# Windowed attention feeding a SwiGLU block: two groups moved one unit, one output from the PE to the crossbar, and a copy ahead of a load

## The chip, the cores and the metric

The kernel runs on one core of a Trainium2 chip. The metric is the device time of one execution in microseconds (us). The kernel before was run 8 times: median 239.15 us, from 238.8 to 240.25. One execution more was profiled.

The engines are named as in the profile: PE is TensorE (PEld its weight loads), DVE is VectorE, ACT is ScalarE, POOL is GpSimd, SP is SyncE, which here only issues DMAs.

## The reference

Attention over a sink of 4 keys and a causal window of 128 keys, for 4 batches, 8 heads, 768 tokens and a head size of 64; then a SwiGLU block over all 3072 tokens, with 512 model columns and 1536 inner columns. Inputs and output are float32.

```python
def _attn_ref(q, k, v, n_sink, window):
    scores = scale * np.matmul(q, k.transpose(0, 1, 3, 2))
    keep = is_sink | in_window          # key < 4, or 0 <= query - key < 128
    scores = np.where(keep, scores, -1000000000.0)
    a = np.exp(scores - np.max(scores, axis=-1, keepdims=True))
    a = a / (np.sum(a, axis=-1, keepdims=True) + 1e-09)
    return np.matmul(a, v)

x = attn_out.transpose(0, 2, 1, 3).reshape(B * S, H * D)
g = x @ w_gate
out = (g / (1 + np.exp(-g)) * (x @ w_val)) @ w_out
```

## The kernel before

**Two tilings.** Attention works on 12 *groups* of 256 tokens, three to a batch (`g`, with `b, c = divmod(g, 3)`; `c == 0` is the start of a batch, which has no sink step and no keys before it). The SwiGLU block works on 8 *blocks* of tokens (`tb`) of the sizes 256, 256, 256, 512, 512, 512, 512, 256 (L42). Their first tokens (`OFF`) are 0, 256, 512, 768, 1280, 1792, 2304 and 2816. So block 3 holds groups 3 and 4, block 4 groups 5 and 6, block 5 groups 7 and 8, block 6 groups 9 and 10.

**Steps of attention for a group.** Four loads bring k and q of both 128-token halves as bfloat16 into the tile `nat` (L111, POOL), two bring v into `va` (L122, POOL); the two together are `NV(g)`. From group 4 on `nat` has one buffer (`natp`, L62), so the loads of a group wait until the transposes of the group before have read it. `xbar(g)` (L253) transposes the four pieces by DMA on SP into `kT` and `qT` (L259). For groups 2 and 3 `step_TN` does this on the PE. `step_S` (L277, twice for each group, four heads each) makes 8 to 12 score matmuls (L292) into four PSUM banks, and four exponentials on ACT (L299); its mask multiply on DVE (L304) is put off in the list `later`. `step_K` (L308) makes scores and the exponential against the sink keys. `step_PV` (L338, four for each group: 2 halves of the tokens by 2 halves of the heads) multiplies with v (L355) and puts off a reciprocal (L363) and a multiply (L369) on DVE, which write `xn`. `step_X` (L377, two for each group) transposes `xn` into the block's input `xT`: on the PE with a copy by DVE or ACT for the groups in `PEX` (L45; L396, L403, L399), by a DMA on SP for the others (L391). `flush` (L210) emits what stands in `later`.

**Units of the SwiGLU block.** A `gate` unit (L448) makes the gate matmuls `pg` (L417), the tanh on ACT (L432), then the attention steps woven into it, then the value matmuls `pv` (L417) and two DVE operations, `u` (L438) and `ht` (L444), and flushes. A `down` unit (L462) makes 12 matmuls (L475) for 128 tokens, with the attention steps spread between them and a flush after each, then a copy by ACT (L480) and the output's DMA on SP (L483).

**What sets the order.** Every engine works in program order, and the program order is written out by hand: `weave` (L513) walks over a list of units and hands to unit *i* the steps that `slots` has for it, in the order in which they are listed. SP and POOL issue their DMAs in this order too, and wait at each one until what it needs is there. PSUM has 8 banks in one pool (`psum`, L74), each new tile taking the bank that has been free longest.

The units that the change touches:

- first weave (L654): units 0 to 11 are gates of blocks 0 and 1, 12 to 17 the six gates of block 2, 18 and 19 the downs of block 0, 20 and 21 of block 1, 22 and 23 of block 2. Into units 14 to 22 groups 3 and 4 are woven
- second weave (L677), block 3: units 0 to 11 are its gates, 12 to 15 its downs. Groups 5 and 6 are woven in by `pair(5, 6)` (L669), which places the steps of two groups by unit, all shifted by `sh` where that is given
- the weaves after that (L681, L684) use `pair(7, 8)` and `pair(9, 10)` without a shift

Of the kernel before, what the change touches and what calls it, by code (L numbers as in the profile page):

```python
# [14 lines left out]
def kernel(  # L15
# [12 lines left out]
    nc = tc.nc  # L28
# [13 lines left out]
    SIZES = [256, 256, 256, 512, 512, 512, 512, 256]  # L42
    assert sum(SIZES) == NTOK and NG == 12
    OFF = [sum(SIZES[:i]) for i in range(len(SIZES))]
    PEX = (0, 1, 2, 4)  # L45

    VS = 72
    FCH = [2] * 6
# [108 lines left out]
    warmed = const.tile([P, 1], FP32)  # L157
# [49 lines left out]
    kTs, qTs, es_t, e_t, xns, xTs = {}, {}, {}, {}, {}, {}  # L207
# [171 lines left out]
    def step_X(g, j, evict="v"):  # L379
# [6 lines left out]
        elif tb > 1 and off == 0:  # L386
            xTs[tb] = dense(xtp.tile([P, DMC * 512], BF16, tag="xT", name="xT"),
                            DMC, SIZES[tb])
        if g not in PEX:
            def sp():  # L390
                nc.sync.dma_start_transpose(xTs[tb][:, :, off:off + P], xns[g, j])  # L391
# [97 lines left out]
    def gates(tb):  # L489
        return [(gate, tb, f) for f in range(0, DFC, 512 // SIZES[tb])]  # L490

    def downs(tb):
        return [(down, tb, t) for t in range(SIZES[tb] // P)]

    def A(fn, *a):
        return lambda: fn(*a)

    def TN(g, evict="av"):
        return [A(step_TN, g, i, j, evict) for j in range(2) for i in range(2)]

    def Ss(g):
        return [A(step_S, g, p2) for p2 in range(2)]

    def PVs(g):
        return [A(step_PV, g, j, hh) for hh in range(2) for j in range(2)]

    def Xs(g):
        return [A(step_X, g, j) for j in range(2)]

    def K(g):  # L510
        return A(step_K, g)

    def weave(us, slots):  # L513
        assert all(i < len(us) for i in slots)
        for i, (fn, tb, x) in enumerate(us):
            fn(tb, x, slots.get(i, []))
# [7 lines left out]
    def slots(*pairs):  # L524
        sl = {}
        for at, steps in pairs:
            for i, step in zip(at if isinstance(at, tuple) else (at,) * len(steps),
                               steps):
                sl.setdefault(i, []).append(step)
        return sl  # L530
# [114 lines left out]
    def L(*fs):  # L645
        def f():
            for x in fs:
                x()
        return f

    def NV(g):
        return L(A(load_nat, g), A(load_v, g))

    weave(us, slots(  # L654
        (0, [K(1)]), (1, [A(step_PV, 1, 0, 0), A(step_PV, 1, 0, 1, "a"), A(step_PV, 1, 1, 0),
                              A(step_PV, 1, 1, 1, "a"), flush]),
        (2, [A(step_X, 1, 0, "a"), A(step_X, 1, 1, "now")]),
        ((4, 4, 5, 5), TN(2)), ((6, 7), Ss(2)), (6, [K(2)]),
        ((8, 8), PVs(2)[:2]), (9, [A(step_PV, 2, 0, 1, "a"), A(step_PV, 2, 1, 1, "a")]),
        ((10, 11), [A(step_X, 2, 0, "a"), A(step_X, 2, 1, "a")]),  # L660
        (11, [NV(4), lambda: nc.gpsimd.tensor_copy(out=vcl[64:128], in_=vcl[0:64])]), ((14, 14, 15, 15), TN(3, "aa")),
        (15, [A(xbar, 4)]), (15, [NV(5)]), (19, [A(xbar, 5)]), (19, [NV(6)]),
        (23, [A(xbar, 6)]), (23, [NV(7)]),
        ((17, 18), Ss(3)), (18, [A(step_ks, 1)]), (18, [A(step_vsb, 1)]),
        ((19, 19, 19, 20), PVs(3)), (20, Xs(3)),
        ((19, 20), Ss(4)), (19, [K(4)]),
        ((21, 21, 22, 22), PVs(4)), (22, Xs(4))))

    def pair(ga, gb, sh=0):  # L669
        s = sh  # L670
        return [((s, s + 2), Ss(ga)), (s, [K(ga)]),
                ((s + 4, s + 5, s + 6, s + 7), PVs(ga)),
                ((s + 6, s + 8), Ss(gb)), ((s + 8, s + 9), Xs(ga)), (s + 6, [K(gb)]),
                ((12, 12, 13, 13) if s else (10, 10, 11, 12), PVs(gb)),
                ((14, 14) if s else (12, 13), Xs(gb))]

    weave(gates(3) + downs(3), slots(  # L677
        (2, [A(xbar, 7)]), (2, [NV(8)]),
        (15, [A(step_ks, 2), A(step_vsb, 2)]), *pair(5, 6),
        (15, [A(xbar, 8)]), (15, [NV(9)])))  # L680
    weave(gates(4) + downs(4), slots(  # L681
        *pair(7, 8), (3, [A(xbar, 9)]), (15, [A(step_ks, 3), A(step_vsb, 3)]),
        (3, [NV(10)]), (15, [A(xbar, 10)]), (15, [NV(11)])))
    weave(gates(5) + downs(5), slots(*pair(9, 10), (6, [A(xbar, 11)])))  # L684
    us = gates(6) + gates(7) + downs(6) + downs(7)
    us[-1] = (lambda tb, t, a: down(tb, t, a, True), *us[-1][1:])
# [37 lines left out]
```

## Time and profile before

| | us |
|---|---|
| median of 8 runs | 239.15 |
| the profiled execution | 238.8 |
| its span, first to last instruction | 236.9 |
| PE busy | 229.1 |
| DVE busy | 158.6 |
| ACT busy | 114.6 |
| POOL busy | 74.5 |

The profiled execution lies at the low end of the 8 runs; its span is 1.9 us shorter than its time. The table of windows gives the engines by stage. Each row has the stretch in us from the span's start, its length, the busy time and number of instructions of each engine, the granted clock of the PE, the busy share of DMA (not used here), and the GB/s moved.

```profile
43.25:55.16 11.91, 11.91 (x120) 10.46 (x120) 8.41 (x14) 6.13 (x12) 4.73 (x6) 1.00 2.10 152
55.16:75.37 20.21, 19.80 (x179) 10.10 (x181) 11.85 (x33) 9.63 (x21) 8.05 (x10) 1.00 1.18 123
75.37:101.53 26.16, 25.85 (x198) 12.48 (x201) 22.03 (x44) 14.72 (x30) 9.46 (x12) 1.00 1.45 143
101.53:111.27 9.74, 9.69 (x53) 4.55 (x53) 3.12 (x10) 1.79 (x3) 3.50 (x5) 1.00 1.85 187
```

The five busy columns are PE, PEld, DVE, ACT and POOL. The first row is units 12 to 17 of the first weave, the second its downs, the third the gates of block 3, the fourth its downs. The PE is busy in all of them, at the full clock. DVE is busiest in the gates, 22.03 of 26.16 us.

### The profile page before, as it was taken

To read this page: it belongs to the slowest core of one execution; us is meant where nothing else is said; L and a number is where in the kernel's file an instruction comes from. 1 tells how busy PE (TensorE), PEld (TensorE's weight loads), DVE (VectorE), ACT (ScalarE), POOL (GpSimd) and SP (SyncE) were. 2 spreads that over 40 slices of the span, in tenths; PEclk is the share of its full clock that TensorE was granted. 3 is DMA by queue.
4 is the path that set the end of the run, shared out by engine and by line. 5 is a ranking of instruction groups with operands and counts; after the bars stand their busy time and mean duration, and the time that the engine had idled before them with its cause. 6 is when DMAs were issued, how large, how long until landed. Compare 5 with 4: busy or idle time off the path is not lost.

```text
span 236.9 us, 4886 instructions
## 1 busy us (share of the span) xinstructions
PE 229.1 (97%) x1874; PEld 127.3 (54%) x1901; DVE 158.6 (67%) x335; ACT 114.6 (48%) x237; POOL 74.5 (31%) x98
## 2 busy tenths in 40 slices
PE   8899999999999999999999999999999999999994
PEld 5567845795554444544445454444554445488443
DVE  5998788768652888960898980698970598877000
ACT  5796485467452836412846522655622663333221
POOL 8995875720807126170260800080000000000000
DMA  8999999993999989999499994599214100200132
GB/s 140 155 179 178 180 200 206 158 149 73 134 136 201 174 114 117 150 117 220 112 113 130 104 80 153 135 90 140 43 21 142 59 3 0 44 3 1 52 127 89
DMA packets 107655, 27.36 MB, mean 115 GB/s; under 512 B 94704, under 2 KB 104688, under 8 KB 107632
## 3 DMA queue, kind: packets, MB, share of 16 engines
q0 software_dynamic: 76640, 13.90, 77.1%
q1 hardware_dynamic: 30448, 12.89, 26.7%
q8 instruction: 15, 0.25, 0.4%
q10 hardware_dynamic: 544, 0.26, 0.4%
q14 instruction: 8, 0.07, 0.1%
HBM read 28.34 MB, written 6.29 MB: 146 GB/s over the span
## 4 chain that ended last, share of the span: by engine, by line
PE 88%; ACT 4%; DVE 2%; DMA 2%; issue 2%; POOL 0%; DVEq 0%; ACTq 0%; POOLq 0%
PE pd L475 26%; PE pv L417 26%; PE pg L417 25%; PE o L355 4%; PE s L292 4%; DMA x<-in_q_dram 2%; ACT e L299 2%; PE pn L245 1%; ACT xn L366 1%; ACT e L572 1%; PE o L335 1%; PE pk L320 1%; ACT th L432 1%; DVE u L438 1%; PE px L396 0%
## 5 line engine op out<-in xcount | busy, mean ns | idle before, releaser
L438 DVE SCALAR_TENSOR_TENSOR u<-th,pg 128x512 bf16<-128x512 f32 x72 | 49.1, 682 | 38.7 <-ACT th L432 38.7
L417 PE MATMUL pg<-xT,wg 128*128 128x512 bf16 (+1 forms) x351 | 73.1, 335 | 0.7
L417 PE MATMUL pv<-xT,wv 128*128 128x512 bf16 (+1 forms) x351 | 73.0, 336 | 0.7 <-ACT e L299 0.2
L432 ACT ACTIVATE th<-pg 128x512 f32<-128x512 f32 x72 | 43.5, 603 | 62.3 <-PE pg L417 58.5
L475 PE MATMUL pd<-wo,ht 128*128 128x512 bf16 (+2 forms) x291 | 64.8, 370 | 0.4
L444 DVE TENSOR_TENSOR ht<-u,pv 128x512 bf16<-128x512 bf16 x66 | 45.4, 687 | 10.4 <-PE pv L417 3.5
L417 PEld LDWEIGHTS <-wg 128*128 128x128 bf16 x360 | 35.0, 98 | 28.1 <-issue 0.7
L299 ACT ACTIVATE e<-s 128x512 bf16<-128x512 f32 (+1 forms) x88 | 42.7, 581 | 3.5 <-PE s L292 3.5
L475 PEld LDWEIGHTS <-ht 128*128 128x128 bf16 x300 | 27.9, 98 | 30.0 <-issue 0.5
L417 PEld LDWEIGHTS <-wv 128*128 128x128 bf16 x360 | 32.0, 98 | 20.9 <-issue 1.7
L111 POOL DMA_DIRECT2D nat<-in_k_dram x20 | 17.6, 888 | 75.2 <-DMA qT<-nat 72.9
L480 ACT ACTIVATE ot<-pd 128x512 f32<-128x512 f32 (+1 forms) x24 | 14.3, 596 | 47.4 <-PE pd L475 43.4
L304 DVE TENSOR_TENSOR e<-e,mask 128x1024 bf16<-128x1024 bf16 (+1 forms) x44 | 27.4, 657 | 3.9 <-ACT e L299 3.9
L122 POOL DMA_DIRECT2D va<-in_v_dram x24 | 21.5, 914 | 5.4 <-DMA wo<-in_moe_w_out_dram 2.5
L369 DVE TENSOR_TENSOR xn<-o,rcp 128x256 bf16<-128x256 f32 x44 | 18.7, 424 | 1.5
L355 PEld LDWEIGHTS <-e 128*128 128x128 bf16 x352 | 15.0, 98 | 8.0 <-DVE lt L603 0.4
L111 POOL DMA_DIRECT2D nat<-in_q_dram x20 | 17.7, 899 | 1.0 <-DMA wv<-in_moe_w_val_dram 0.4
L355 PE MATMUL o<-va,e 128*128 128x65 bf16 x352 | 17.0, 193 | 0.4 <-DVE lt L603 0.3
L292 PE MATMUL s<-qT,kT 64*128 64x128 bf16 (+1 forms) x240 | 12.9, 237 | 0.0
L292 PEld LDWEIGHTS <-kT 64*128 64x128 bf16 x240 | 7.7, 94 | 7.6 <-issue 6.6
L482 DVE TENSOR_SCALAR ot<-pd 128x128 f32<-128x128 f32 x1 | 0.3, 291 | 14.3 <-PE pd L475 14.3
L363 DVE RECIPROCAL rcp<-o 128x4 f32<-128x4 f32 x48 | 8.1, 174 | 1.4 <-PE o L355 1.3
(73 smaller groups left out, 91.9 us busy)
## 6 DMA issues: line engine op xcount, KB each, us to landing
out_dram<-ot SPq DMA_DIRECT2D x23, 256.0 KB
va<-in_v_dram POOLq DMA_DIRECT2D x24, 128.0 KB, 6.4
nat<-in_k_dram POOLq DMA_DIRECT2D x20, 128.0 KB, 5.1
nat<-in_q_dram POOLq DMA_DIRECT2D x20, 128.0 KB, 5.7
wg<-in_moe_w_gate_dram POOLq DMA_DIRECT2D x6, 256.0 KB, 7.8
wv<-in_moe_w_val_dram POOLq DMA_DIRECT2D x6, 256.0 KB, 8.6
wo<-in_moe_w_out_dram POOLq DMA_DIRECT2D x4, 384.0 KB, 11.1
st<-in_q_dram ACTq DMA_DIRECT2D x2, 128.0 KB
```

Of the source, the lines that this page charges most:

```text
L111: nc.gpsimd.dma_start(x[:, i, j].rearrange("p (h d) -> p h d", d=D), src[b, :, t0:t0 + P].rearrange("h p d -> p h d"))
L122: nc.gpsimd.dma_start(va[:, j, :, 0:D], v[b, :, t0:t0 + P].rearrange("h p d -> p h d"))
L292: nc.tensor.matmul(pss[2 * pp + h][:, col:col + n], kTs[b][r, p, kk:kk + P], qTs[b][r, p, qq:qq + n], start=True, stop=True)
L299: nc.scalar.activation(e_t[g][:, h0 + h, lo:512], pss[2 * pp + h][:, lo:512], AF.Exp, scale=scale)
L304: nc.vector.tensor_tensor(e, e, m[:, :, lo:512].broadcast_to([P, 2, 512 - lo]), op=ALU.mult)
L355: nc.tensor.matmul(o, l, r, start=(c == 0 and i == 0), stop=(i == len(mms) - 1), skip_group_check=True)
L369: nc.vector.tensor_tensor(xn, po[:, :, 0:D], rcp.broadcast_to([P, 4, D]), op=ALU.mult)
L417: nc.tensor.matmul(ps[:, i * n:(i + 1) * n], ws[fi][:, c, fo * P:(fo + 1) * P], xTs[tb][:, c], start=(c == 0), stop=(c == DMC - 1))
L432: nc.scalar.activation(th, pg, AF.Tanh, scale=0.5)
L438: nc.vector.scalar_tensor_tensor(u, th, 1.0, pg, op0=ALU.add, op1=ALU.mult)
L444: nc.vector.tensor_tensor(hts[tb][:, f:f + 512 // SIZES[tb]].rearrange("p a n -> p (a n)"), u, pv, op=ALU.mult)
L475: nc.tensor.matmul(po, hts[tb][:, f, ts * P:(ts + 1) * P], wos[f // n][:, f % n, lo:hi], start=(f == 0), stop=(f == DFC - 1))
```

## The change

It has four parts.

1. `PEX` loses group 4: its output goes to `xT` by two DMA transposes on SP instead of eight PE transposes and two DVE copies.
2. In the first weave the scores, PVs and outputs of groups 3 and 4 stand one unit sooner (scores at units 16 and 17, then 18 and 19). K(4) now stands behind group 4's second scores. `xbar(5)` and `NV(6)` move from unit 19 to unit 22.
3. `xbar(6)` and `NV(7)` move from unit 23 of the first weave to unit 1 of the second, `xbar(7)` from unit 2 to unit 8 of the second, `NV(8)` from unit 2 to unit 13. Groups 5 and 6 are woven in with a shift of one unit, where `pair` now gives other places for the second group's PVs (10, 11, 11, 12) and outputs (12, 13).
4. Ahead of `NV(8)` stand a flush and `behind(3)`: POOL copies one element of `xTs[3]`, in its last column, to the scratch tile `warmed`.

```diff
--- before.py
+++ after.py
@@ -42,7 +42,7 @@
     SIZES = [256, 256, 256, 512, 512, 512, 512, 256]
     assert sum(SIZES) == NTOK and NG == 12
     OFF = [sum(SIZES[:i]) for i in range(len(SIZES))]
-    PEX = (0, 1, 2, 4)
+    PEX = (0, 1, 2)
 
     VS = 72
     FCH = [2] * 6
@@ -506,6 +506,10 @@
 
     def Xs(g):
         return [A(step_X, g, j) for j in range(2)]
+
+    def behind(tb):
+
+        nc.gpsimd.tensor_copy(out=warmed[0:1], in_=xTs[tb][0:1, 0, 511:512])
 
     def K(g):
         return A(step_K, g)
@@ -659,25 +663,24 @@
         ((8, 8), PVs(2)[:2]), (9, [A(step_PV, 2, 0, 1, "a"), A(step_PV, 2, 1, 1, "a")]),
         ((10, 11), [A(step_X, 2, 0, "a"), A(step_X, 2, 1, "a")]),
         (11, [NV(4), lambda: nc.gpsimd.tensor_copy(out=vcl[64:128], in_=vcl[0:64])]), ((14, 14, 15, 15), TN(3, "aa")),
-        (15, [A(xbar, 4)]), (15, [NV(5)]), (19, [A(xbar, 5)]), (19, [NV(6)]),
-        (23, [A(xbar, 6)]), (23, [NV(7)]),
-        ((17, 18), Ss(3)), (18, [A(step_ks, 1)]), (18, [A(step_vsb, 1)]),
-        ((19, 19, 19, 20), PVs(3)), (20, Xs(3)),
-        ((19, 20), Ss(4)), (19, [K(4)]),
-        ((21, 21, 22, 22), PVs(4)), (22, Xs(4))))
+        (15, [A(xbar, 4), NV(5)]),
+        ((16, 17), Ss(3)), (18, [A(step_ks, 1), A(step_vsb, 1)]),
+        ((18, 18, 18, 19), PVs(3)), (19, Xs(3)),
+        ((18, 19), Ss(4)), (19, [K(4)]),
+        ((20, 20, 21, 21), PVs(4)), (21, Xs(4)), (22, [A(xbar, 5), NV(6)])))
 
     def pair(ga, gb, sh=0):
         s = sh
         return [((s, s + 2), Ss(ga)), (s, [K(ga)]),
                 ((s + 4, s + 5, s + 6, s + 7), PVs(ga)),
                 ((s + 6, s + 8), Ss(gb)), ((s + 8, s + 9), Xs(ga)), (s + 6, [K(gb)]),
-                ((12, 12, 13, 13) if s else (10, 10, 11, 12), PVs(gb)),
-                ((14, 14) if s else (12, 13), Xs(gb))]
+                ((10, 11, 11, 12) if s else (10, 10, 11, 12), PVs(gb)),
+                ((12, 13), Xs(gb))]
 
     weave(gates(3) + downs(3), slots(
-        (2, [A(xbar, 7)]), (2, [NV(8)]),
-        (15, [A(step_ks, 2), A(step_vsb, 2)]), *pair(5, 6),
-        (15, [A(xbar, 8)]), (15, [NV(9)])))
+        (1, [A(xbar, 6), NV(7)]), (8, [A(xbar, 7)]), *pair(5, 6, 1),
+        (13, [flush, A(behind, 3), NV(8)]),
+        (15, [A(step_ks, 2), A(step_vsb, 2), A(xbar, 8), NV(9)])))
     weave(gates(4) + downs(4), slots(
         *pair(7, 8), (3, [A(xbar, 9)]), (15, [A(step_ks, 3), A(step_vsb, 3)]),
         (3, [NV(10)]), (15, [A(xbar, 10)]), (15, [NV(11)])))
```

## The prediction

> **What bounds the kernel now.** I read the page first (busy shares, chain of waits), then TensorE's order of time around the change, then the orders of time of SyncE and GpSimd, last the completion marks of the transfers (16 for each transfer in the trace).
>
> ```profile
> span 236.9 us, 4886 instructions
> PE 229.1 (97%) x1874; PEld 127.3 (54%) x1901; DVE 158.6 (67%) x335; ACT 114.6 (48%) x237; POOL 74.5 (31%) x98
> PE 88%; ACT 4%; DVE 2%; DMA 2%; issue 2%; POOL 0%; DVEq 0%; ACTq 0%; POOLq 0%
> ```
>
> TensorE is the chain, and "busy" alone doesn't prove it full, so I looked at starts. From 43 us on a 128x512 matmul follows the last one every 0.216 us; the steps of attention between them cost what they cost. I found two real stalls: 0.17 us after group 6's scores at 89.28 us and 0.24 us at 126.26 us. So what a reordering can still win is TensorE work taken out, plus at most 0.4 us.
>
> ```profile
> 71.25 0.39 PE L396 MATMUL px<-ident,xn 128*128 128x128 bf16 x4
> 71.47 0.59 PE L475 MATMUL pd<-wo,ht 128*128 128x512 bf16 x2
> 71.91 0.39 PE L396 MATMUL px<-ident,xn 128*128 128x128 bf16 x4
> 72.13 3.40 PE L475 MATMUL pd<-wo,ht 128*128 128x512 bf16 x14
> 75.37 1.03 PE L417 MATMUL pg<-xT,wg 128*128 128x512 bf16 x4
> 89.28 0.50 PE L292 MATMUL s<-qT,kT 64*128 64x256 bf16 x8
> 111.27 1.03 PE L417 MATMUL pg<-xT,wg 128*128 128x512 bf16 x4
> ```
>
> Group 4's two PE transposes hold TensorE from 71.25 to 71.47 and from 71.91 to 72.13: 0.22 us each. 75.37 is unit 0 of the weave of block 3, 111.27 that of block 4.
>
> ```profile
> 62.97 1.21 SPq L259 DMA_TRANSPOSE kT<-nat  x1
> 64.84 1.27 SPq L259 DMA_TRANSPOSE qT<-nat  x1
> ...
> 69.45 3.49 SPq L391 DMA_TRANSPOSE xT<-xn  x2
> ...
> 105.16 1.25 SPq L391 DMA_TRANSPOSE xT<-xn  x1
> ```
>
> SyncE issues in order, about 1.3 us for each transpose. Group 3's output waits behind group 5's four input transposes, which wait for loads.
>
> ```profile
> 59.10 1.75 POOL L111 DMA_DIRECT2D nat<-in_k_dram  x2 [9.61 <-DMA qT<-nat]
> 72.57 1.75 POOL L111 DMA_DIRECT2D nat<-in_k_dram  x2 [8.21 <-DMA qT<-nat]
> 87.62 1.76 POOL L111 DMA_DIRECT2D nat<-in_k_dram  x2 [9.81 <-DMA qT<-nat]
> 99.78 1.75 POOL L111 DMA_DIRECT2D nat<-in_k_dram  x2 [6.89 <-DMA qT<-nat]
> ```
>
> There is one `nat` buffer. A group's loads start when the last transpose of the group before has landed; these four lines are one chain, 13.5, 15.1 and 12.2 us a step. By the marks group 4's transposes land at 58.55, group 5's at 72.01, group 6's at 87.07, group 7's at 98.94, about 0.55 us ahead of each line.
>
> **What the Trainium skill says.** "DMA: Bandwidth & Descriptors", section "Issuing engines are not separate DMA queues": transfers of all queues share the same 16 DMA engines. The trace agrees: with nothing beside it a 128x512 transpose lands 2.4 us after its issue (140.13 to 142.53); group 6's second output transpose, issued at 105.16 with group 8's six loads ahead, takes 6.0 and lands at 111.15, 0.12 us before TensorE wants it. "TensorE: Matmul & The Clock Gate", "Part 4: PE-mode transpose", gives about 275 ns for one in a kernel; here the records last 219 ns but follow each other every 56, and 56 is what is saved. "Perfetto Trace Analysis", "DMA Instruction — SWDGE (GPSIMD)": a GpSimd DMA's record ends with its descriptors, not the data; so I use marks for landings (3.4 to 7.5 us after issue for loads here), not the 0.9 us records.
>
> **The change, part by part.**
>
> *Group 4's output by the crossbar.* Eight PE transposes go: 8 x 0.055 = -0.44 us on the path. Two vector copies of 0.42 us go too, beside TensorE, worth nothing. Two SyncE transposes come: 1.2 us each to issue, 2.4 to land.
>
> *Groups 3 and 4 a unit sooner.* TensorE's work stays. Units 16 and 17 each take one score step of group 3 (0.53 us), so unit 18 starts at 55.16 + 0.53 = 55.69 us. Its six steps put group 4's first scores at matmul 10: 55.69 + 10 x 0.216 + 0.12 + 0.25 + 0.12 (PVs) + gaps of 0.1 = 58.45, against 60.82 before. They need group 4's last transpose, landed at 58.55: 0.1 us of stall. ScalarE then has 4 exps (2.06 us), the output copy (0.6), 4 exps, and only then the exp of K(4), which now stands after the second scores: 59.05 + 2.06 + 0.5 + 2.4 + 0.17 = about 64.2, while TensorE reaches the sink matmuls of PV(4) at about 64.07: another 0.2 with the handover. Masks (0.55 and 0.69 us) and PSUM banks free up ahead of need.
>
> Group 4's last xn is ready near 68.9, its transposes issue at 68.3 and 69.6 and land by 72; unit 0 of block 3 comes at 75.37 - 0.44 + 0.3 = about 75.1. Three us spare: hidden.
>
> *Group 5's crossbar from unit 19 to 22.* On SyncE it now follows unit 21's output (ScalarE copy at about 70.5, issue to 71.4). Its `nat` is there long before, so four issues 1.31 apart, 71.45 to 75.4, plus 2.45 in a quiet stretch: landed at 77.85. Group 5's scores are moved a unit too, to unit 1: 75.1 + 1.73 + 0.96 = 77.8 (0.96 from 75.37 to 76.33). Level: 0 to 0.5, I take 0.15. Behind the waiting scores stand unit 1's other matmuls, then ScalarE and VectorE.
>
> *Loads and crossbar of groups 6 and 7.* GpSimd starts group 6's loads at 77.85 + 0.55 = 78.4, 5.8 us later than before. A quiet chain step from start of loads to the last landing is 11.3 us (87.62 to 98.94), the others 12.9 and 14.5. With 12.1 group 6 lands at 90.5. Its scores move only from unit 6 to 7: 89.28 - 0.44 + 0.3 + 1.73 = 90.85 or a little after. Stall 0 to 2.0 (14.5 gives 92.9); I take 0.15. Group 7: 91.05 + 12 = 103, needed at 112. Group 5's output on SyncE goes out behind it, at 100.9 to 103.4 instead of 97.5 to 100, needed at 111.2: hidden.
>
> *PVs of group 6.* One moves from unit 10 to 11, so its reciprocal and multiply (0.55 us) stand behind the last `ht` instead of before it. VectorE is nearly full from 82 to 103 us. The shifted work leaves it about 0.2 us later at unit 2, and 0.55 less lies before `ht`'s end at 102.67: no loss, perhaps 0.2 won or lost.
>
> *The GpSimd copy.* `behind(3)` reads column 511 of `xTs[3]`. Group 6's tokens start at 1536 and belong to block 4; block 3 holds groups 3 and 4. So the copy waits for group 4's output, landed 30 us earlier, and holds nothing: some 0.1 us of GpSimd (a 64x195 copy took 0.34), beside everything. Queued behind it are group 8's loads, which wait anyway for group 7's transposes: about 103.6 instead of 99.78. Group 6's last output transpose, issued near 105.5, then has three loads ahead of it, not six: landed 109 to 110.5 instead of 111.15. Slack grows from 0.1 to about 1 us. Group 8's crossbar, after unit 14's output (109.92 before), still finds its data; after it the schedule is unchanged.
>
> Sum against the profiled execution (span 236.9, 238.8 with what lies around it): -0.44 + 0.1 + 0.2 + 0.15 + 0.15 = +0.16, 238.96. The median of the runs shown is 0.35 above that execution, 239.15; they spread to 240.25, which I put partly to edges like 111.15 against 111.27. That edge gets wider, so I carry 0.15 of the 0.35 over: 239.1.
>
> **Rivals.** *A, all edges hold:* -0.44, the stall at 89.28 (0.17) gone as well, and the spread at 111 gone: 238.8 - 0.6 + 0.1 = 238.3. For it: each new wait was costed at only 0.1 to 0.2. Against it: four of them lie within 0.2 us of need. *B, group 6's operands are late:* one mechanism, the single-buffer chain. Its start moves 5.8 us, TensorE's need only 1.6. From 12.5 us a step on, TensorE stands at group 6's scores; with 14.5, group 6's own step before, it stands 2.0, against the 0.15 counted: 239.1 + 1.9 = 241.0. For it: two of three steps took 12.9 and more. Against it: those had outputs or earlier loads in flight, now fewer. *C, the hold that holds nothing:* group 8's loads again delay group 6's output to 112, 0.8 us late: 239.9. Against it: they start later than before.
>
> **Numbers.** Own forecast 0.42 (238.7 to 239.8), A 0.20, B 0.28 (240 to 241.5), C 0.10 (239.6 to 240.2). Range 238.3 to 241.0, leaving out half of B. No change is within 0.3% (0.7 us), about what a measurement of this kernel can tell. Faster: A and a touch of the first, 0.22; slower: B and some of C, 0.32; the same 0.46.
>
> **What will show it.** No L396 at 71 us, two more L391 issues before 71. Scores of group 5 near 77.8 and of group 6 near 90.9: a gap ahead of them named a DMA wait means B. GpSimd's copy with no wait ahead, and group 8's loads following group 7's landing and not group 6's output. If GpSimd is seen waiting there for a later transpose, my reading of block 3 is wrong; if TensorE stops at unit 0 of block 3 or 4, the landings of outputs are.

## The result, and the profile after

| | before | after |
|---|---|---|
| median (runs), us | 239.45 (32) | 242.18 (11) |
| lowest to highest, us | 238.54 to 241.24 | 239.93 to 245.39 |
| the profiled execution, us | 238.8 | 241.45 |
| its span, us | 236.9 | 239.6 |
| ratio after / before, 95% interval | | 1.0099 (1.0074 to 1.0124) |

The changed kernel is slower by 1.0%, some 2.4 us. (Ratios compare the two kernels run in turn on one chip; this one leaves out the two slowest runs of the changed kernel, 244.52 and 245.39 us, which the median keeps, so it lies below the quotient of the medians.)

From the page of the kernel after: the span, the busy time of each engine, and the chain that ended last by engine.

```profile
span 239.6 us, 4881 instructions
PE 229.5 (96%) x1866; PEld 127.5 (53%) x1893; DVE 156.8 (65%) x333; ACT 114.8 (48%) x237; POOL 74.7 (31%) x99
PE 76%; DVE 7%; DMA 7%; SPq 3%; POOL 3%; issue 3%; ACT 1%; DVEq 0%; POOLq 0%; ACTq 0%
```

TensorE has eight matmuls fewer, and its busy time is not longer (229.5 against 229.1). What changed is the chain: TensorE's share falls from 88 to 76%, the DMAs' rises from 2 to 7%, and the issue queue of SyncE (SPq) appears in it with 3%. So time was lost in stops, and the stops end on transfers. (VectorE's share rises too, from 2 to 7%: the chain passes over its last `xn` operations, which end at 105.42 us. SyncE was still busy with earlier issues then, so they are not the cause.) TensorE's order of time after the change says where. The columns are start, duration, engine, line, operation and count; the bracket is the idle time ahead and what ended it.

```profile
75.36 1.03 PE L417 MATMUL pg<-xT,wg 128*128 128x512 bf16 x4
...
79.44 0.56 PE L292 MATMUL s<-qT,kT 64*128 64x256 bf16 x10 [1.16 <-DMA qT<-nat]
...
92.34 0.50 PE L292 MATMUL s<-qT,kT 64*128 64x256 bf16 x8
...
114.04 1.04 PE L417 MATMUL pg<-xT,wg 128*128 128x512 bf16 x4 [1.27 <-DMA xT<-xn]
```

75.36 is unit 0 of block 3, and 114.04 unit 0 of block 4, as 75.37 and 111.27 were before. The scores at 79.44 are the third of their step: two stand ahead of the stop, at 78.05. Up to unit 0 of block 3 nothing is lost. Within block 3 there are two stops: at group 5's scores, waiting for group 5's transposes, and ahead of block 4, waiting for group 6's output. Group 6's scores at 92.34 show none. The account of the two profiled executions by start marks (a stop is longer there than the idle time in brackets, since the ends of matmuls are modelled):

| stretch | before | after | difference |
|---|---|---|---|
| start to gates of block 2 | 43.25 | 43.49 | +0.24 |
| those gates to unit 0 of block 3 | 32.12 | 31.87 | -0.25 |
| block 3 | 35.90 | 38.68 | +2.78: +1.36 at group 5's scores, +1.43 ahead of block 4 |
| unit 0 of block 4 to the end | 125.66 | 125.56 | -0.10 |
| span | 236.93 | 239.60 | +2.67 |

The first row lies ahead of anything that the change moved; why the two profiles differ there I did not study. The windows of block 3 say the same by engine. Columns are as before (stretch, length, PE, PEld, DVE, ACT, POOL, clock, DMA share, GB/s). The downs begin at 102.00 us, so the first row holds the gates and the start of the downs, the second the rest of the downs. (In the table of before, where the downs begin at 100.66, the split at 101.53 lies within them too; rows of the two tables can't be compared one by one.)

```profile
75.36:104.32 28.96, 27.49 (x211) 13.37 (x214) 23.21 (x46) 14.93 (x30) 10.68 (x13) 1.00 1.43 126
104.32:114.04 9.72, 8.40 (x40) 3.63 (x38) 1.80 (x10) 2.39 (x4) 5.26 (x6) 1.00 1.15 141
```

TensorE now lacks 1.5 us in the first and 1.3 in the second, at the full clock. VectorE is no busier over the block than before (25.01 us against 25.15).

Why the transfers are late is seen in the queues that issue them. SyncE's order of time after the change, first around group 5, then around group 6's output:

```profile
62.36 2.61 SPq L391 DMA_TRANSPOSE xT<-xn  x2
...
68.65 3.58 SPq L391 DMA_TRANSPOSE xT<-xn  x2
72.33 0.53 SPq L483 DMA_DIRECT2D out_dram<-ot  x1
72.96 1.23 SPq L259 DMA_TRANSPOSE kT<-nat  x1
...
101.47 1.22 SPq L259 DMA_TRANSPOSE qT<-nat  x1
102.79 4.37 SPq L391 DMA_TRANSPOSE xT<-xn  x3
107.69 0.34 SPq L483 DMA_DIRECT2D out_dram<-ot  x1
108.14 1.30 SPq L391 DMA_TRANSPOSE xT<-xn  x1
```

Group 3's output (62.36) now goes out among group 5's loads, and by its completion marks takes 7.0 and 7.9 us to land. Group 4's output (68.65) holds the queue for 3.58 us, its second issue alone for 2.29, and group 5's four input transposes start behind it at 72.96, where I had 71.45. Their last lands at 79.40, and TensorE resumes at 79.44.

GpSimd's order of time after the change:

```profile
79.95 1.75 POOL L111 DMA_DIRECT2D nat<-in_k_dram  x2 [15.24 <-DMA qT<-nat]
...
92.88 1.75 POOL L111 DMA_DIRECT2D nat<-in_k_dram  x2 [7.68 <-DMA qT<-nat]
...
98.18 0.18 POOL L512 CAST warmed<-xT 1x1 f32<-1x1 bf16 x1
106.81 1.75 POOL L111 DMA_DIRECT2D nat<-in_k_dram  x2 [8.45 <-DMA qT<-nat]
```

The copy (L512) has no wait: it runs at 98.18, in 0.18 us, right behind group 7's loads. Group 8's first load then waits only for group 7's transposes (`qT<-nat`) and starts at 106.81, while group 6's second output transpose is not yet issued (108.14). That one lands at 113.99, 5.85 us later, and unit 0 of block 4 starts at 114.04.

### The profile page after: what moved, and what is told of

Same layout as the page of the kernel before. It is cut to its first block, busy times and chain, and to the rows that moved or that the text cites. A ratio compares the mean times of both kernels' runs of the same rounds, so it can differ in the third digit from the quotient of the medians.

```text
span 239.6 us, 4881 instructions
## 1 busy us (share of the span) xinstructions
PE 229.5 (96%) x1866; PEld 127.5 (53%) x1893; DVE 156.8 (65%) x333; ACT 114.8 (48%) x237; POOL 74.7 (31%) x99
## 4 chain that ended last, share of the span: by engine, by line
PE 76%; DVE 7%; DMA 7%; SPq 3%; POOL 3%; issue 3%; ACT 1%; DVEq 0%; POOLq 0%; ACTq 0%
PE pv L417 24%; PE pg L417 23%; PE pd L475 19%; PE o L355 4%; PE s L292 4%; DMA wg<-in_moe_w_gate_dram 3%; DMA xT<-xn 2%; DVE xn L369 2%; SPq L259 2%; DVE u L438 2%; SPq L391 2%; DVE ht L444 1%; DMA qT<-nat 1%; POOL rows L100 1%; DVE e L304 1%
```

## The experiments

Two theories to begin with, one for each stop. **The hold (H):** the stop ahead of block 4 comes from group 8's loads being in flight under group 6's last output transpose, and the copy doesn't prevent it because it reads block 3 (groups 3 and 4) and not block 4 (groups 5 and 6). Its rival: that transpose is late because it is issued 3 us later than before (108.14 against 105.16), and holding the loads would change little or make group 8 late. **SyncE's order (S):** the stop at group 5's scores comes from group 4's output transposes, which now stand on SyncE ahead of group 5's input transposes. Its rival is the move of group 5's transposes from unit 19 to 22, late whatever stands ahead. The question under both was whether the two stops add up.

**1. The copy on the right block** (`e1_hold4`, the changed kernel with one figure changed):

```diff
-        (13, [flush, A(behind, 3), NV(8)]),
+        (13, [flush, A(behind, 4), NV(8)]),
```

> The copy reads block 4's input (group 6's last columns) in place of block 3's, so it holds group 8's loads till group 6's output has landed. Theory H (the hold of the change holds nothing, and group 8's loads delay group 6's output): GpSimd waits at the copy for a transfer of xT, group 8's loads start after 110 us instead of at 106.8, group 6's second output transpose lands 2.4 to 3 us after its issue instead of 5.85, TensorE's stop of 1.43 us ahead of unit 0 of block 4 shrinks below 0.3, the stop of 1.36 us at group 5's scores stays; time 1.1 to 1.5 us under the changed kernel's (about 240.4, ratio to before near 1.004). Rival Q (SyncE's order, with group 7's four transposes ahead of the outputs of groups 5 and 6, is what makes group 6's output late): the stop stays above 1 us and the time near 241.8.

Measured: median 239.33 us (22 runs), ratio to before 1.0010 (0.9998 to 1.0021). Its orders of time, GpSimd first, then TensorE:

```profile
110.79 0.18 POOL L512 CAST warmed<-xT 1x1 f32<-1x1 bf16 x1 [12.47 <-DMA xT<-xn]
111.82 1.76 POOL L111 DMA_DIRECT2D nat<-in_k_dram  x2 [0.86 <-DMA out_dram<-ot]
```

```profile
79.48 0.56 PE L292 MATMUL s<-qT,kT 64*128 64x256 bf16 x10 [1.08 <-DMA qT<-nat]
...
112.65 1.03 PE L417 MATMUL pg<-xT,wg 128*128 128x512 bf16 x4
```

Now the copy waits 12.47 us for `xT<-xn`, and the loads start at 111.82. Group 6's transpose is issued at 108.29, as late as in the changed kernel, but lands in 2.44 us instead of 5.85, and block 4 starts without a stop. So the rival of H is out: the late issue is still there and costs nothing. The stop at group 5's scores is still there too, so it is a separate matter. One figure gives back 2.1 of the 2.4 us that were lost, more than the 1.1 to 1.5 that I had expected. Why more came back than the stop of 1.43 us was not tried. The profiled execution (239.97 us) is the third slowest of its 22, so its stop at group 5's scores need not be that of the others.

**2. No copy at all** (`e2_nocopy`):

```diff
-        (13, [flush, A(behind, 3), NV(8)]),
+        (13, [flush, NV(8)]),
```

> The changed kernel without the GpSimd copy, all else left. Theory H: the copy never waited, so group 8's loads start where they did (one chain step after group 7's transposes landed), both stops of TensorE stay at 1.0 to 1.5 us each and the time is that of the changed kernel within 0.3% (241 to 242). Rival: the copy held the loads a little, then they start over 0.5 us earlier and the stop ahead of block 4 grows.

Measured: median 241.57 us (4 runs, the profiled one 243.6), ratio 1.0093 (1.0072 to 1.0114), which can't be told from the one with the copy on block 3. Group 8's loads start at 105.46, again one step of the chain behind group 7's; group 6's transpose, issued at 107.54, takes 7.01 us. So the copy as changed did nothing. But the two stops did not stay as I had expected. TensorE's order of time in this run, which also shows what can follow a stop:

```profile
78.18 0.87 PE L292 MATMUL s<-qT,kT 64*128 64x128 bf16 x12
...
114.60 1.04 PE L417 MATMUL pg<-xT,wg 128*128 128x512 bf16 x4 [2.79 <-DMA xT<-xn]
115.56 0.92 PE L292 MATMUL s<-qT,kT 64*128 64x128 bf16 x12
116.41 0.41 PE L320 MATMUL pk<-qT,kss 128*32 128x128 bf16 x8
116.75 1.89 PE L417 MATMUL pv<-xT,wv 128*128 128x512 bf16 x4
```

The stop at group 5's scores has shrunk to 0.3 us by start marks, and the one ahead of block 4 has grown to 2.79. The edit can't have done the first, since it comes 20 us later. What differs is that group 4's input transposes happened to land 2.6 us sooner (56.25 against 58.90), and so group 5's loads started 2.6 us sooner (56.81 against 59.46). Group 3's output, issued behind them, then landed in 4.3 and 3.4 us instead of 7.0 and 7.9. Group 4's two output transposes were issued in 1.2 us each, and group 5's first input transpose at 72.00 instead of 72.96. So the stop at group 5's scores varies from one execution to the next. The four value matmuls at 116.75 take 1.89 us, where such a group takes 1.03.

**3. Group 4 back on the PE** (`e3_pex4`, the changed kernel with two SyncE issues fewer and eight PE transposes more):

```diff
-    PEX = (0, 1, 2)
+    PEX = (0, 1, 2, 4)
```

> The changed kernel with group 4's output back on TensorE (8 transposes, 0.44 us), all else left. Theory S (group 4's two output transposes on SyncE, stretched by group 5's loads, push group 5's input transposes back): group 5's first input transpose issues about 1.5 us sooner, near 71.4 instead of 72.96, its last lands near 77.8, the stop at group 5's scores falls from 1.36 to below 0.3 us; net of the 0.44 us, 0.6 to 0.9 us faster than the changed kernel if the stop ahead of block 4 stays as it is. Rival P (the place at unit 22 is late by itself, since it stands behind unit 21's output): the first issue moves by less than 0.5 us and the stop stays over 0.8 us, so the time rises by 0.3 to 0.4.

Measured: median 241.23 us (4 runs), ratio 1.0105 (1.0071 to 1.0139). Group 5's first input transpose issues at 71.62 instead of 72.96, its last lands at 77.98 instead of 79.40, and the stop at group 5's scores is gone, as S says. But this profile alone doesn't prove S: here too group 5's loads had started early (56.66), as in experiment 2, where the stop was nearly gone with group 4's transposes on SyncE. The time is no shorter, which I had not expected. TensorE's order of time shows where it went:

```profile
91.56 0.51 PE L292 MATMUL s<-qT,kT 64*128 64x256 bf16 x8 [0.30 <-DMA qT<-nat]
...
113.66 1.02 PE L417 MATMUL pg<-xT,wg 128*128 128x512 bf16 x4 [1.83 <-DMA xT<-xn]
```

The stop ahead of block 4 grew from 1.27 to 1.83 us. With group 5 sooner, the chain of loads runs sooner too: group 8's start at 105.05 and group 6's transpose, issued at 106.94, takes 6.67 us. Block 4 starts when that transpose lands, and this is not set by TensorE. A stop removed ahead of it is only moved into it, here as in experiment 2.

**4. Both** (`e4_pex4_hold4`: edits 1 and 3):

```diff
-    PEX = (0, 1, 2)
+    PEX = (0, 1, 2, 4)
...
-        (13, [flush, A(behind, 3), NV(8)]),
+        (13, [flush, A(behind, 4), NV(8)]),
```

> Both edits: group 4's output on TensorE, and the copy reading block 4's input. Theories H and S together: no stop of TensorE over 0.3 us at group 5's scores or ahead of block 4; time 0.1 to 0.3 us beside that of the kernel before (239.2 to 239.8). Rivals Q or P: one of the stops stays, 240.3 or more.

Measured: median 238.93 us (13 runs), ratio 0.9994 (0.9984 to 1.0004). No stop for a DMA is left in block 3; block 4 starts at 111.36, as before the change (111.27). Group 5's loads started at 58.35 here and group 3's output was slow again (6.7 and 6.3 us to land), yet group 5's first input transpose was issued at 71.52. So slow transfers alone don't delay it, with group 4 off SyncE, and experiment 2 shows that group 4's two issues alone hardly do: counted from the first down matmul of block 0 that issue comes at 15.73 us in experiments 2, 3 and 4, against 17.01 in the changed kernel. The delay takes both, and the place at unit 22 isn't late by itself. Once the loads are held, taking the first stop away counts (0.4 us against experiment 1); the rest of what it gives is spent on the eight PE transposes.

**5. Group 5's scores later** (`e5_s_later_hold4`: edit 1, and the first scores of groups 5 and 6, with their sink step, at units 2 and 8 instead of 1 and 7, so that they come when the transposes have landed near 79.4):

```diff
-        return [((s, s + 2), Ss(ga)), (s, [K(ga)]),
+        return [((2 * s, s + 2), Ss(ga)), (2 * s, [K(ga)]),
...
-                ((s + 6, s + 8), Ss(gb)), ((s + 8, s + 9), Xs(ga)), (s + 6, [K(gb)]),
+                ((2 * s + 6, s + 8), Ss(gb)), ((s + 8, s + 9), Xs(ga)), (2 * s + 6, [K(gb)]),
```

> The hold on block 4, and the first scores (with the sink scores) of group 5 at unit 2 instead of 1, of group 6 at unit 8 instead of 7; group 4's output by the crossbar as in the change. If the stop at group 5's scores (1.1 to 1.4 us) is only that they stand a unit ahead of their transposes, it goes: group 5's scores come near 79.7, its last transpose near 79.4, group 6's scores near 92.8 against a landing near 92.2, and the 0.44 us of TensorE work saved shows: 238.4 to 238.8, ratio 0.997 to 0.999. Rival: VectorE, nearly full in block 3, gets its masks later and TensorE stops for it near unit 11 or 12; then 239.2 or more.

Measured: median 238.2 us (22 runs), ratio 0.9969 (0.9954 to 0.9984): faster than both kernels. The scores stand at 79.55 without a stop and block 4 starts at 110.87. In its profiled execution (239.5 us) the old stop shows up a block later, as TensorE's order of time has it:

```profile
110.87 1.03 PE L417 MATMUL pg<-xT,wg 128*128 128x512 bf16 x4
...
149.22 1.04 PE L417 MATMUL pg<-xT,wg 128*128 128x512 bf16 x4 [1.14 <-DMA xT<-xn]
```

149.22 is unit 0 of block 5. Group 10's loads start at 138.34, ahead of group 8's two outputs, which take 5.26 and 7.55 us to land. Only 3 of the 22 runs took over 239 us, this one among them, so most may well go without this stop.

**6. Group 4's output by the crossbar in the kernel before, nothing else** (`e6_before_pex3`):

```diff
-    PEX = (0, 1, 2, 4)
+    PEX = (0, 1, 2)
```

> The kernel before with one part of the change alone: group 4's output by the crossbar. Its xn are ready near 71, its two transposes follow group 3's on SyncE at about 73 and 74.3 and land near 76.8, against a need at 74.9: TensorE stops 1.5 to 2 us at unit 0 of block 3, and saves 0.44: ratio 1.004 to 1.007. Rival (the landing is hidden anyway): no stop, ratio 0.998.

Measured: median 247.48 us (4 runs), ratio 1.0358 (1.0324 to 1.0392). The orders of time of SyncE, GpSimd and TensorE:

```profile
74.15 3.88 SPq L391 DMA_TRANSPOSE xT<-xn  x2
```

```profile
72.58 1.76 POOL L111 DMA_DIRECT2D nat<-in_k_dram  x2 [7.87 <-DMA qT<-nat]
```

```profile
84.00 1.86 PE L417 MATMUL pg<-xT,wg 128*128 128x512 bf16 x4 [8.61 <-issue]
```

Group 4's transposes go out at 74.15 and 76.11 under group 6's loads and land at 81.58 and 83.91, after 7.43 and 7.80 us; TensorE stops 8.61 us ahead of block 3. (The view names no transfer as the end of this wait, only "issue"; the second landing, 0.09 us ahead of the start, ties it to one.) I had expected less than a quarter of that. In the changed kernel, with groups 3 and 4 a unit sooner and group 6's loads later, the same two transposes land at 74.39 and 74.83, ahead of their need at 75.36. Which of the two moves makes the crossbar usable for group 4 was not tried.

**7. The hold alone in the kernel before** (`e7_before_hold4`: group 8's loads from unit 2 to unit 13, behind a copy from block 4):

```diff
-        (2, [A(xbar, 7)]), (2, [NV(8)]),
+        (2, [A(xbar, 7)]),
...
+        (13, [flush, A(behind, 4), NV(8)]),
```

> The kernel before with group 8's loads at unit 13 behind a copy that reads block 4's input. Group 6's second output transpose lands 2.4 us after its issue at 105.2, near 107.6 instead of 111.15; group 8's loads start near 108.2 instead of 99.8, its input transposes are done near 120, needed near 125. TensorE didn't stop there in the profile of before, so the profiled span stays within 0.2 us; if the spread of the runs of before (238.5 to 240) comes from this edge, the median falls by 0.1 to 0.4 us and the spread narrows (ratio 0.998 to 1.000). Rival: group 8's transposes become late, ratio over 1.002.

Measured: median 239.06 us (13 runs, 238.8 to 240.4), ratio 1.0012 (0.9996 to 1.0028). Group 6's transpose falls from 6.0 to 2.43 us (105.27 to 107.70), and nothing is gained, since it had landed 0.12 us in time before. Nor is the spread of the runs narrower, so that edge doesn't explain it.

**8. Another order instead of a hold** (`e8_xbar7_later`: the copy stays on block 3; group 7's transposes move from unit 8 to unit 11, which frees SyncE ahead of the outputs and should delay group 8's loads):

```diff
-        (1, [A(xbar, 6), NV(7)]), (8, [A(xbar, 7)]), *pair(5, 6, 1),
+        (1, [A(xbar, 6), NV(7)]), *pair(5, 6, 1), (11, [A(xbar, 7)]),
```

> The changed kernel, its idle copy left as it is, with group 7's four input transposes at unit 11 instead of 8, so behind group 5's output on SyncE. Theory H (what counts is that group 8's loads are not in flight under group 6's output): the loads can only start once group 7's transposes have landed, near 109, after group 6's second output transpose has issued (near 108); that lands before 112.3 and the stop ahead of block 4 falls from 1.4 to 3 us to below 0.5, without any hold; time 239.3 to 240.3. Rival Q (the order on SyncE sets it whatever the loads do): the same number of transposes stand ahead of group 6's output, so its stop stays above 1 us.

Measured: median 239.08 us (12 runs), ratio 1.0001 (0.9984 to 1.0018). The loads start at 107.08, sooner than I expected; the stop is gone all the same. SyncE's order of time, then GpSimd's:

```profile
107.00 1.23 SPq L391 DMA_TRANSPOSE xT<-xn  x1
```

```profile
107.08 1.76 POOL L111 DMA_DIRECT2D nat<-in_k_dram  x2 [8.79 <-DMA qT<-nat]
```

The transpose leads the loads by 0.08 us, where it followed them by 1.33, and lands in 3.71 us instead of 5.85, at 110.72; block 4 starts at 112.27 with no stop. The transpose is also issued 1.14 us sooner than in the changed kernel, so this run alone doesn't separate the two theories; experiment 1 does. The time lies just under the range that I had given.

**9. Two holds** (`e9_two_holds`: experiment 5, and group 10's loads behind a copy from block 5):

```diff
-        (3, [NV(10)]), (15, [A(xbar, 10)]), (15, [NV(11)])))
+        (13, [flush, A(behind, 5), NV(10)]), (15, [A(xbar, 10)]), (15, [NV(11)])))
```

> e5 (scores of groups 5 and 6 a unit later, hold on block 4) and the same hold once more: group 10's loads at unit 13 of the next weave, behind a copy that reads block 5's input. In the profile of e5 those loads were in flight under group 8's output (5.3 and 7.55 us to land, TensorE stopped 1.14 us ahead of block 5). Theory H (loads in flight under an output's transpose): that output lands about 2.4 us after its issue, no stop over 0.3 us is left in the trace, profiled span 236.2 to 236.6, median 237.9 to 238.3 and runs closer together, ratio 0.995 to 0.997. Rival: group 10's transposes, now at 149 to 155 us, come late for its scores near 161 and the time rises over 238.5.

Measured: median 238.44 us (7 runs, 237.97 to 238.7), ratio 0.9963 (0.9946 to 0.9981). GpSimd's order of time:

```profile
110.94 0.18 POOL L512 CAST warmed<-xT 1x1 f32<-1x1 bf16 x1 [13.30 <-DMA xT<-xn]
...
144.39 0.18 POOL L512 CAST warmed<-xT 1x1 f32<-1x1 bf16 x1 [13.68 <-DMA xT<-xn]
```

Both copies wait for the output that they are to protect, and group 8's second output lands in 2.44 us (141.82 to 144.26), against 7.55 in experiment 5. Blocks 4 and 5 start without a stop. The median lies just over the 237.9 to 238.3 that I had expected, and the ratio can't be told from experiment 5's; both beat the kernel before by about 0.3%.

**10. Scores later, the copy on block 3** (`e10_s_later_only`: the score edit of experiment 5 alone on the changed kernel):

```diff
-        return [((s, s + 2), Ss(ga)), (s, [K(ga)]),
+        return [((2 * s, s + 2), Ss(ga)), (2 * s, [K(ga)]),
...
```

> The changed kernel, its idle copy on block 3 as it is, with only the first scores of groups 5 and 6 a unit later: the stop at group 5's scores (0.3 to 1.4 us) goes. If the two stops were independent, the time would fall by what that stop was, to about 240.5. Theory H: group 8's loads and group 6's output land by the chain of loads and not by TensorE, so what TensorE gains ahead it waits for at block 4: that stop grows to 2.5 us or more and the time stays at 241 to 242 (ratio 1.008 to 1.011).

Measured: median 242.5 us (4 runs, 241.1 to 245.54), ratio 1.0141 (1.0103 to 1.0179), above the 1.008 to 1.011 that I had expected, with an interval that overlaps the changed kernel's. The stop at group 5's scores is gone and the one ahead of block 4 is longer by more than that, in TensorE's order of time:

```profile
113.67 1.04 PE L417 MATMUL pg<-xT,wg 128*128 128x512 bf16 x4 [2.88 <-DMA xT<-xn]
```

This is experiment 3 by another way: block 4 starts at 113.67 here, 113.66 there and 114.04 in the changed kernel, whatever was gained ahead of it (114.60 in experiment 2). The score edit that wins with the hold wins nothing without it.

The table puts the runs side by side: group 6's second output transpose, and group 8's loads.

| kernel | transpose issued | first load of group 8 | us to land | landed |
|---|---|---|---|---|
| before | 105.16 | 99.78 | 6.0 | 111.15 |
| after | 108.14 | 106.81 | 5.85 | 113.99 |
| no copy | 107.54 | 105.46 | 7.01 | 114.55 |
| group 4 on the PE | 106.94 | 105.05 | 6.67 | 113.61 |
| scores later only | 106.29 | 104.88 | 7.33 | 113.62 |
| group 7's transposes later | 107.00 | 107.08 | 3.71 | 110.72 |
| copy on block 4 | 108.29 | 111.82 | 2.44 | 110.73 |
| two holds | 108.33 | 111.98 | 2.56 | 110.89 |

In the other runs with a hold on block 4 (experiments 4, 5 and 7) it lands in 2.43 to 2.57 us. Where loads were in flight ahead of it for over a microsecond (the kernels before and after, no copy, group 4 on the PE, scores later only), the completion marks show one thing more: it lands with the last load issued ahead of it, within 0.5 us. In the kernel before these marks are 110.88 for the load and 111.15 for the transpose, in the changed kernel 113.59 and 113.99, and in experiment 10 113.70 and 113.62. In experiment 10 the loads start 1.9 us sooner than in the changed kernel and the last one ahead still lands no sooner, after 7.94 us; why is not shown.

## Why the prediction was wrong

I predicted no change (239.1 us, 238.3 to 241.0); the kernel is about 2.4 us slower. Point by point:

*The step that failed* is in the part on the GpSimd copy: "Group 6's last output transpose, issued near 105.5, then has three loads ahead of it, not six: landed 109 to 110.5 instead of 111.15. Slack grows from 0.1 to about 1 us." Both terms were wrong. It was issued at 108.14, since group 7's input transposes hold SyncE up to 102.69 and the third of group 5's and 6's output transposes comes out only at 105.96. This alone would have cost nothing (experiment 1: issued at 108.29, no stop). The time in flight is what cost the stop, and it doesn't scale with the loads issued ahead: two ahead cost 5.85 us (and 7.33 in experiment 10), and the three that I had counted on cost 7.01 and 6.67 (experiments 2 and 3), where six ahead had cost 6.0. Of those six, two had landed by 105.16 us, when the transpose was issued, which my count left out. The table's split is between 2.4 to 2.6 us with the loads held back and 5.85 to 7.33 with loads started over a microsecond ahead. The Trainium skill's "DMA: Bandwidth & Descriptors", section "Issuing engines are not separate DMA queues", which I had cited for all queues sharing the 16 DMA engines, bears on exactly this; the runs agree with it, and I drew a proportion from it that neither it nor the trace gave. I had read rightly that `behind(3)` holds nothing (0.18 us, no wait), and then argued that nothing needed holding.

*Rival C was the mechanism,* with the wrong size (0.8 us where 1.27 to 2.88 were measured) and a chance of 0.10. My argument against it, that the loads start later than before, looked at the wrong pair of times: what counts is their start against the issue of the transpose, and that had moved as well. Experiments 1 and 2 show it from both sides.

*Group 5's crossbar* was the second term off: landed 77.85 predicted, 79.40 measured; a stop of 0.15 taken, 1.36 measured, beyond the bound of 0.5. I had let SyncE go on at 71.45, and overlooked that group 3's output, moved a unit sooner, falls among group 5's loads, and that group 4's second issue takes 2.29 us rather than 1.2. My price of about 1.3 us an issue had overlooked a line that I showed: the two issues at 69.45 take 3.49 us, 2.19 of them the first. (A slip in the sum is small beside this: 75.37 - 0.44 + 0.3 is 75.23, not 75.1.) The delay is gone in the profile of experiment 2, where group 3's output landed soon, and in that of experiment 4, where group 4's two issues were off SyncE. That the slow output is what holds up the issues behind it is read from the traces alone, and its size isn't explained: in experiment 10 the output was slow and group 4 on SyncE, and group 5's first issue came at 15.88 us after the first down matmul, only 0.15 later. In the profiles that keep these scores at unit 1 and group 4 on SyncE (the changed kernel, experiments 1, 2 and 8) the stop is 1.36, 1.28, 0.27 and 0.92 us, so 1.36 is the largest seen.

*Rival B did not come.* Group 6's chain step was 12.2 us (79.95 to 92.15) against 12.1 taken; its scores at 92.34 follow from one unit (1.73) and the 1.36 of group 5's stop, with no wait of their own.

*What held:* the eight PE transposes, -0.44, of which -0.25 is left net up to block 3, so about 0.2 of small stops rather than the 0.3 I took. Group 4's output stayed hidden, though with 0.5 us to spare and not 3 (74.83 against 75.36). VectorE cost nothing. From unit 0 of block 4 on, the schedule runs as before (125.56 against 125.66). With the copy on block 4 the time is 1.0010 of before, which is what I had forecast for the change as it stands; that agreement is luck, since the profile of that run still has a stop that my sum had at 0.15 us.

*The sum* treated the stops as separate terms. They aren't: block 4 starts when group 6's output lands, and without a hold this stayed between 113.6 and 114.6 us, whatever TensorE had gained ahead of it (experiments 2, 3 and 10).

Some things stay open: why the loads in flight take as long as they do, and these two. The spread of the kernel before isn't explained by the edge at 111 us (experiment 7), so the 0.15 that I carried over for it had no ground. And of the runs of the changed kernel, those above 243 us show a mean granted clock of TensorE of 0.986 to 0.993, the others 0.998 to 1.0: stops seem to cost clock in some executions; what decides it was not tried.

## What to carry to other kernels

A transpose that stands just ahead of a block must be compared with the loads that are issued near it, by the time of each, not by how many there are: in the profile of experiment 8 a lead of 0.08 us, instead of 1.33 us behind, went with no stop. A copy that reads a tile's last column can hold a queue until that tile is complete, but only if it reads the tile that is about to be needed: look for its wait in the trace, since a hold with no wait ahead of it holds nothing. Where a stop ends on a transfer among loads, as here ahead of block 4, removing an earlier stop can gain nothing until that one is gone. And a stop in one profile can be a matter of that execution: compare it across the profiles of kernels that are alike up to there, before an experiment is said to have removed it.

## What the runs showed of the hardware

A DMA transpose of 128x512 takes 2.4 us alone. Beside the loads of one group, output transposes took up to 7.9 us (group 3's in the changed kernel; experiment 6's two 7.43 and 7.80), and one input transpose 9.4 (experiment 10, issued at 109.42). Issues on SyncE can back up as well: most transposes take 1.2 to 1.3 us to issue, but with transfers in flight one took 2.19 (the kernel before, at 69.45), one 2.29 and one 2.73 (the changed kernel, at 69.95 and 111.26).

A stop can cost more than itself. The windows of experiment 2 and of experiment 6 after their stops, columns as above, the clock third from the end:

```profile
110.00:120.00 10.00, 7.16 (x42) 2.87 (x42) 2.01 (x4) 3.47 (x8) 0.71 (x1) 0.83 1.72 189
```

```profile
83.70:90.00 6.30, 6.00 (x37) 2.49 (x38) 2.34 (x4) 3.38 (x7) 2.38 (x3) 0.70 0.84 143
```

The means of 0.83 and 0.70 hide a clock of one half: by the traces' clock records it was halved from 115.73 to 119.14 us in experiment 2, just after a stop of 2.79 us, and from 80.66 to 87.48 in experiment 6, within and after the stop of 8.61. In experiment 2 the matmuls from 114.60 to 119.65 took 5.05 us where the same ones took 3.48 in the changed kernel (114.04 to 117.52): 1.6 us more. Experiment 10's stop of 2.88 us cost no clock in its profile. The Trainium skill's "TensorE: Matmul & The Clock Gate", section "Why this matters for your kernels", warns of idle gaps of TensorE over about 3 us. These runs show a loss already at 2.79 and none at 2.88, so the length of the stop alone doesn't decide. Its place may: in every trace that records several changes of the clock, they lie a whole number of 3.41 us apart (here 3.41 and 6.83). In experiment 2 TensorE stood for 2.3 us of the 3.41 that ended in the change; in experiment 10, counted on from its first change, a period ends at 112.38 and splits the stop into 1.75 and 1.3 us. Two traces don't prove this.
